# Attention decode gradients on one core: which DMA engines carry the rows of eight gradient stores

## The chip, the core and the metric

The kernel runs on one core of a Trainium2 chip. A core has a matrix engine (TensorE, PE in the profile, with its weight loads as PEld), a vector engine (VectorE, DVE), a scalar engine (ScalarE, ACT), a general engine (GpSimd, POOL), a queue engine (SyncE, SP) and 16 DMA engines that move data between the chip's memory (HBM) and the core's own memory of 128 partitions. SP and POOL issue DMAs here: SP's go through the queue that the profile names q1, POOL's through q0, and both queues feed the same 16 DMA engines.

The metric is the time on the device in microseconds, as the median of several runs. A profile of one execution shows its span, which is from the first to the last instruction.

## What is computed

For 2 x 32 = 64 heads, one query row attends to 8192 keys of 128 numbers in bf16. The reference takes the output and the gradients of q, k and v:

```
def _fwd_reference(q, k, v):
    scale = q.shape[-1] ** -0.5
    scores = jnp.einsum("bhqd,bhkd->bhqk", q, k) * scale
    p = _softmax(scores, axis=-1)
    return jnp.einsum("bhqk,bhkd->bhqd", p, v)
...
    _out, _vjp = jax.vjp(_f, q, k, v)
    _grads = _vjp(grad_out)
```

For one head that is, with the probabilities p and the incoming gradient g: the output p v; dv = p times g (an outer product, 8192 x 128); dp = v g; ds = p (dp - sum(p dp)); dq = scale ds k; dk = scale ds times q (again an outer product, 8192 x 128). K and V are read once (268 MB in all) and dk and dv are written once (268 MB).

## The kernel before

**Tiles.** Each head's K and V is one tile of 128 partitions, in which a partition holds 64 consecutive rows of 128 numbers, 16 KB. Twelve such tiles fit (`NTILE`, line 19), so six heads are in flight. `slot_of` (line 78) says which of the twelve places a tile takes: that of the tile which the head six places before it used, so `load(58, 0)`, K of head 58, goes where V of head 52 was, and `load(57, 1)` where K of head 51 was.

**Work on a head.** A tile is worked on in four chunks of 16 x 128 columns. PE transposes a chunk (line 184), ACT copies the result out (line 186), PE takes its product with q or with the incoming gradient (line 195). The softmax steps follow on DVE and ACT, PE sums up output and dq from the untransposed tiles (line 339), and then DVE writes dv over the V tile and dk over the K tile, chunk by chunk (`outer`, line 394). When the last chunk of a tile is done, its 2 MB are stored to HBM. The heads overlap: a step of the main loop holds transposes of one head and outer products of heads before it. dv of a head comes first, then dk of the same head four steps later, then dv of the next head. The order of instructions on each engine is fixed by the program (`pin`).

**Loads and stores.** All loads of K and V are issued by SP in that order (line 98). A load into a place waits, in SP's queue, until the store of the tile that used the place before has landed. Whole stores are issued by POOL (line 412) as one DMA of 128 rows; only the last head's go in quarters on SP. A whole load or store puts eight rows of 16 KB on each of the 16 DMA engines.

**Split stores.** `by_rows` (line 83) issues one store as several DMAs, each with a number of rows given in a list. In the kernel before, the dk stores of the eight heads in `SPREAD` (line 21: heads 4, 11, 18, 25, 32, 39, 46 and 53) go as 126 rows and 2 rows (line 409). At the start line 108 sets the place of POOL's DMAs among the engines back, and then a DMA of six rows of q is issued (line 110, `FIRST`). In the trace's list of packets each split store puts nine rows on fourteen engines and one row on the two others, in the place of eight on all sixteen; the change's words call these two engines 4 and 5.

Of the kernel before, what the change touches and what calls it, by code (L numbers as in the profile page):

```python
# [17 lines left out]
NG = 2  # L18
NTILE = 12
FIRST = 6  # L20
SPREAD = range(4, 60, 7)

@with_exitstack
def kernel(
# [12 lines left out]
    B, H, Sq, D = q.shape  # L38
    Sk = k.shape[2]
    P = nc.NUM_PARTITIONS  # L40
# [3 lines left out]
    NT = Sk // P  # L44
# [5 lines left out]
    load_eng = nc.sync  # L50
    store_eng = nc.gpsimd
    pin = tc.keep_in_program_order
# [30 lines left out]
    def by_rows(eng, dst, src, rows):  # L83

        p = 0
        for m in rows:
            pin(eng.dma_start(out=dst[p : p + m], in_=src[p : p + m], max_dma_last_dim=NT * D))
            p += m
# [15 lines left out]
    for w, a in enumerate((q, grad_out)):  # L104
        rows = a.rearrange("b h s d -> (b h s) d")
        r0 = FIRST if w == 0 else 0
        if r0:
# [3 lines left out]
                    out=qd_nat[:r0, w, :], in_=rows[:r0], max_dma_last_dim=D  # L111
# [276 lines left out]
    def outer(i, w, c, ends):  # L388

        h = heads[i]  # L390
        n0 = c * CH
        shape = [P, CH, D // 2, 2]
        pin(
            nc.vector.tensor_tensor(  # L394
                out=h.tile[w][:, n0 : n0 + CH, :].rearrange("p n (e t) -> p n e t", t=2),
                in0=h.qb[w][:]
                .rearrange("p (e t) -> p e t", t=2)
                .unsqueeze(1)
                .to_broadcast(shape),
                in1=h.pair[w][:, n0 : n0 + CH, :].unsqueeze(2).to_broadcast(shape),  # L400
                op=ALU.mult,
            )
        )
        if c + 1 in ends:
            at = ends.index(c + 1)
            b0, b1 = (ends[at - 1] if at else 0) * CH, (c + 1) * CH
            dst = (dv_v if w else dk_v)[i]
            if w == 0 and i in SPREAD:
                by_rows(store_eng, dst, h.tile[w], (P - 2, 2))
            else:  # L410
                eng = load_eng if len(ends) > 1 else store_eng
                pin(eng.dma_start(out=dst[:, b0:b1, :], in_=h.tile[w][:, b0:b1, :]))  # L412
# [10 lines left out]
    for g in range(SL * BH + O0 + NCH + 4 - SL):  # L423
# [15 lines left out]
        if x := within(O1):  # L439
            outer(x[0], 1, x[1], last if x[0] == BH - 1 else whole)  # L440
        if x := within(O0):
            outer(x[0], 0, x[1], last if x[0] == BH - 1 else whole)
        ev = None
        if g < SL * BH:
            i, r = divmod(g, SL)
# [74 lines left out]
```

## Time and profile before

| what | value |
|---|---|
| runs | 1284.86, 1285.96 and 1285.71 us, median 1285.71 |
| the profiled execution's own time | 1284.86 us |
| its span | 1283.1 us |
| PE, PEld, DVE, ACT busy | 88%, 67%, 73%, 76% of the span |
| POOL busy | 6% |
| HBM read and written | 268.47 MB and 268.47 MB, 418 GB/s over the span |
| whole stores by POOL (line 412) | 118, median 68.0 us from issue to landing |
| loads of a whole tile by SP (line 98) | 127, median 19.4 (V) and 19.7 us (K) |
| split stores by POOL (line 87) | 8 of 2016 KB (73.2 us) and 8 of 32 KB (72.6 us) |
| last head's stores by SP (line 412) | 8 of 512 KB, 22.1 us |

The time of a run is somewhat longer than the span, since it also holds what lies before the first and after the last instruction. Shares of busy time are means over the whole span. "From issue to landing" contains the time that a transfer waits behind others in its queue. The queues q8 and q14 carry the engines' own instructions.

### The profile page before, as it was taken

The page shows a single profiled execution, that of the slowest core. Times are in us where ns is not written, and L with a number is a line of the kernel's source. Part 1 is how long each engine was busy: PE and PEld are TensorE (multiplying, and loading weights), DVE is VectorE, ACT ScalarE, POOL GpSimd, SP SyncE. Part 2 cuts the span into 40 slices and gives each one's busy share as a digit, 9 for nine tenths or more (in the row PEclk, how much of TensorE's full clock was granted, in tenths as well). Part 3 has the DMA queues.
Part 4 walks back from the last instruction along what each step waited for, and adds up shares of the span by engine and source line. Part 5 has one row for each costly group of instructions (what it writes and reads, how often), then busy time and mean ns, then how long its engine had stood idle before and what let it go on. Part 6 is the DMA issues. An engine that isn't in the chain of part 4 may idle for free.

```text
span 1283.1 us, 42576 instructions
## 1 busy us (share of the span) xinstructions
PE 1128.5 (88%) x19268; PEld 859.1 (67%) x19268; DVE 935.2 (73%) x2122; ACT 975.2 (76%) x641; POOL 76.0 (6%) x143
## 2 busy tenths in 40 slices
PE   6999999999988998898889898898889888989881
PEld 5777777667666766676666676676667666667650
DVE  2888888778777777686777687786767677777773
ACT  6888888778877877787777787786778677778750
POOL 0000000000000000000000000000000000000000
PEclk9999999999999999998999999998989899899985
DMA  9999999999999999999999999999999999999996
GB/s 388 422 428 426 428 426 427 428 428 425 428 428 425 418 427 428 428 421 427 428 426 425 426 429 428 425 425 429 427 425 421 423 427 428 423 425 426 428 409 267
DMA packets 40194, 539.68 MB, mean 421 GB/s; under 512 B 5196, under 2 KB 5196, under 8 KB 6476
## 3 DMA queue, kind: packets, MB, share of 16 engines
q1 hardware_dynamic: 20172, 272.70, 50.0%
q0 software_dynamic: 19840, 264.25, 48.8%
q8 instruction: 150, 2.46, 0.7%
q14 instruction: 32, 0.26, 0.0%
HBM read 268.47 MB, written 268.47 MB: 418 GB/s over the span
## 4 chain that ended last, share of the span: by engine, by line
DMA 33%; another core or an unknown queue 29%; PE 16%; issue 10%; DVE 8%; ACT 1%; SPq 1%; POOL 1%; POOLq 0%; DVEq 0%; ACTq 0%
DMA kvt<-in_v_dram 20%; DMA out_dram<-kvt 7%; PE tp L184 7%; DVE kvt L394 5%; DMA kvt<-in_k_dram 5%; PE acc L339 4%; PE dpw L195 2%; PE sw L195 2%; DVE sel L362 1%; ACT ev L186 1%; SPq L98 1%; DMA qd_nat<-in_q_dram 1%; PE dpw L282 1%; POOL out_dram L412 0%
## 5 line engine op out<-in xcount | busy, mean ns | idle before, releaser
L186 ACT COPY ev<-tp 128x2048 bf16<-128x2048 bf16 x512 | 954.4, 1865 | 268.8 <-PE tp L184 256.8
L184 PE MATMUL tp<-ident_bf,kvt 128*128 128x128 bf16 x8192 | 558.5, 223 | 96.6 <-DMA kvt<-in_v_dram 74.4
L394 DVE TENSOR_TENSOR kvt<-qb,pair 128x2048 bf16<-128x2048 bf16 x512 | 621.2, 1214 | 0.3
L184 PEld LDWEIGHTS <-kvt 128*128 128x128 bf16 x8192 | 489.8, 101 | 103.6 <-DMA kvt<-in_v_dram 77.8
L195 PEld LDWEIGHTS <-ev 128*128 128x128 bf16 x8192 | 243.2, 96 | 208.7 <-issue 149.1
L339 PE MATMUL acc<-kvt,dS_pad 128*64 128x512 bf16 x1024 | 166.8, 408 | 0.8 <-DVE dqT L379 0.8
L339 PE MATMUL acc<-kvt,E_pad 128*64 128x512 bf16 x1024 | 160.5, 394 | 0.0
L195 PE MATMUL dpw<-qdT,ev 128*128 128x1 bf16 x4096 | 140.7, 164 | 18.8 <-DVE qb L177 18.0
L362 DVE SCALAR_TENSOR_TENSOR sel<-acc,diag,sel 128x128 f32<-128x128 f32 x384 | 134.7, 351 | 13.6
L195 PE MATMUL sw<-qdT,ev 128*128 128x1 bf16 x4096 | 141.8, 164 | 1.2 <-ACT ev L186 1.2
L207 DVE TENSOR_REDUCE mp<-sw 128x1 f32<-128x64 f32 x64 | 14.4, 224 | 156.1 <-PE sw L195 156.1
L412 POOL DMA_DIRECT2D out_dram<-kvt x118 | 63.3, 536 | 1086.1 <-DVE kvt L394 818.4
L339 PEld LDWEIGHTS <-dS_pad 128*64 128x64 bf16 x1024 | 37.4, 110 | 24.4 <-issue 5.3
L247 DVE CAST E_pad<-E_f 128x64 bf16<-128x64 f32 x64 | 12.5, 195 | 54.5 <-ACT E_f L238 54.5
L339 PEld LDWEIGHTS <-E_pad 128*64 128x64 bf16 x1024 | 36.4, 108 | 21.3 <-issue 0.7
L376 PE MATMUL acc<-ones,sel 128*128 128x1 f32 x256 | 43.5, 239 | 6.2 <-DVE sel L362 6.2
L253 DVE CUSTOM_DVE_ANT_0 junk<-E_f,dpw 128x64 bf16<-128x64 f32 x64 | 14.1, 221 | 45.3 <-PE dpw L195 45.3
L282 PE MATMUL dpw<-ld,ones 128*128 128x1 f32 x256 | 46.3, 250 | 0.1
L376 PEld LDWEIGHTS acc<-ones,sel 128*128 128x128 f32 x256 | 39.3, 194 | 7.3 <-DVE sel L362 7.3
L356 DVE TENSOR_SCALAR sel<-acc,diag 128x128 f32<-128x128 f32 x128 | 44.1, 344 | 0.0
L177 DVE CAST qb<-dpw 128x128 bf16<-128x128 f32 x128 | 35.4, 277 | 6.2 <-PE dpw L168 6.2
L282 PEld LDWEIGHTS dpw<-ld,ones 128*128 128x128 f32 x256 | 38.2, 188 | 0.5 <-DVE ld L253 0.5
(44 smaller groups left out, 314.2 us busy)
## 6 DMA issues: line engine op xcount, KB each, us to landing
out_dram<-kvt POOLq DMA_DIRECT2D x118, 2048.0 KB, 68.0
kvt<-in_v_dram SPq DMA_DIRECT2D x64, 2048.0 KB, 19.4
kvt<-in_k_dram SPq DMA_DIRECT2D x63, 2048.0 KB, 19.7
out_dram<-kvt POOLq DMA_DIRECT2D x8, 2016.0 KB, 73.2
out_dram<-kvt SPq DMA_DIRECT2D x8, 512.0 KB, 22.1
kvt<-in_k_dram SPq DMA_DIRECT2D x2, 512.0 KB, 4.5
kvt<-in_k_dram SPq DMA_DIRECT2D x1, 1024.0 KB, 7.3
out_dram<-kvt POOLq DMA_DIRECT2D x8, 32.0 KB, 72.6
```

Source lines behind the costliest of these rows:

```text
L177: pin(nc.vector.tensor_copy(out=h.qb[w][:], in_=h.qbp))
L184: pin(nc.tensor.transpose(tp[:, t, :], src[:, c * CH + t, :], ident_bf[:]))
L186: pin(nc.scalar.copy(out=ev[:], in_=tp[:]))
L195: nc.tensor.matmul(dst[:, c * CH + t : c * CH + t + 1], lhsT=ev[:, t, :], rhs=qdT[:, w, i : i + 1], start=True, stop=True,)
L207: pin(nc.vector.reduce_max(out=h.mp[:], in_=h.s, axis=AX.X))
L282: nc.tensor.matmul(out, lhsT=ones[:].to_broadcast([P, P]), rhs=col, start=True, stop=True)
L339: nc.tensor.matmul(h.acc[w][g : g + CW, :], lhsT=wts[:, n0 : n0 + CW], rhs=rows[:, n0 : n0 + QT, :].rearrange("p n d -> p (n d)"), start=( ...
L356: nc.vector.tensor_scalar(out=h.sel[:], in0=block, scalar1=diag[:, 0:1], scalar2=None, op0=ALU.mult)
L362: nc.vector.scalar_tensor_tensor(out=h.sel[:], in0=block, scalar=diag[:, b : b + 1], in1=h.sel[:], op0=ALU.mult, op1=ALU.add,)
L376: nc.tensor.matmul(h.acc[w][:, 0:1], lhsT=h.sel[:], rhs=ones[:], start=True, stop=True)
L394: nc.vector.tensor_tensor(out=h.tile[w][:, n0 : n0 + CH, :].rearrange("p n (e t) -> p n e t", t=2), in0=h.qb[w][:] .rearrange("p (e t) -> ...
L412: pin(eng.dma_start(out=dst[:, b0:b1, :], in_=h.tile[w][:, b0:b1, :]))
```

## The change

The number of split dk stores goes from eight to six (heads 5, 14, 23, 32, 41 and 50), each still 126 rows and 2 rows. The dv store of head 52 is split into 9, 95 and 22 rows on POOL and 2 rows on SP; the dv store of head 55 into 95 and 33 rows on POOL. By the words of the change, the 95 rows go to engines 15 and 0 to 3, and the split dk stores leave out engines 4 and 5. All bytes are moved as before, and nothing else differs.

```
-SPREAD = range(4, 60, 7)
+SHIFT = (52, 55)
+SPREAD = range(5, 52, 9)
...
-            if w == 0 and i in SPREAD:
+            if w == 1 and i == SHIFT[0]:
+                by_rows(store_eng, dst, h.tile[w], (9, 95, 22))
+                pin(load_eng.dma_start(out=dst[P - 2 :], in_=h.tile[w][P - 2 :], max_dma_last_dim=NT * D))
+            elif w == 1 and i in SHIFT:
+                by_rows(store_eng, dst, h.tile[w], (95, 33))
+            elif w == 0 and i in SPREAD:
                 by_rows(store_eng, dst, h.tile[w], (P - 2, 2))
```

On POOL's queue the DMAs stand in the order of the code: after the split store of head 50 two whole stores (dv and dk of head 51), then the 9, 95 and 22 rows, five whole stores, the 95 and 33 rows, and whole stores to the end. On SP's queue the store of the last 2 rows of dv of head 52 stands after `load(57, 1)` and before `load(58, 0)`. The other engines' instructions are the same, in the same order.

## The prediction

> **What bounds the kernel now.** First the page's slices and its DMA queues.
>
> ```profile
> span 1283.1 us, 42576 instructions
> ...
> DMA  9999999999999999999999999999999999999996
> ...
> q1 hardware_dynamic: 20172, 272.70, 50.0%
> q0 software_dynamic: 19840, 264.25, 48.8%
> q8 instruction: 150, 2.46, 0.7%
> q14 instruction: 32, 0.26, 0.0%
> ```
>
> The 16 DMA engines are full in 39 of 40 slices, so the kernel is bound by bytes through them, and as they share work unevenly, by the engine that has most. Queue q1 (loads, from SP) moves 272.70 MB in 50.0% of 16 x 1283.1 us: 0.617 us for a row of 16 KB. In the list of packets the median row takes 0.611 us on both queues; I use that. The 150 instruction fetches of q8, 16 KB each, take 0.98 us in the list (147 us in all).
>
> Second, the busy time by windows at the end (the last two columns are the DMA share and GB/s).
>
> ```profile
> 1238.00:1248.00 10.00, 8.45 (x130) 5.99 (x130) 8.53 (x21) 5.90 (x5) 0.53 (x1) 0.96 0.88 372
> 1248.00:1262.00 14.00, 7.37 (x30) 3.08 (x30) 12.63 (x25) 0.00 (x0) 0.00 (x0) 0.50 0.99 414
> 1262.00:1266.00 4.00, 0.00 (x0) 0.00 (x0) 0.04 (x1) 0.00 (x0) 0.00 (x0) 0.50 0.69 285
> 1266.00:1268.00 2.00, 0.00 (x0) 0.00 (x0) 0.00 (x0) 0.00 (x0) 0.00 (x0) 0.50 0.51 213
> 1268.00:1274.00 6.00, 0.00 (x0) 0.00 (x0) 0.00 (x0) 0.00 (x0) 0.00 (x0) 0.50 0.52 217
> 1274.00:1280.00 6.00, 0.00 (x0) 0.00 (x0) 0.00 (x0) 0.00 (x0) 0.00 (x0) 0.50 0.44 180
> 1280.00:1283.00 3.00, 0.00 (x0) 0.00 (x0) 0.00 (x0) 0.00 (x0) 0.00 (x0) 0.50 0.10 36
> ```
>
> All compute ends by 1262. Then a share of 0.69, 0.52 and 0.44 of 16 engines is 11, 8 and 7 engines: seven work to 1280 on stores while nine have run dry. That tail of 18 us is what the change can shorten.
>
> Third, which engines are the seven? The list of packets has start, duration, size and queue, but no engine. On one engine a row starts 3 to 4 ns before the recorded end of the row before it, and each whole transfer puts eight rows and a 4-byte completion on an engine; with both rules the packets chain into 16 lines. Their last packets end at 1279.9 to 1281.0 (seven lines), 1274.4, 1268.1, 1266.2, 1263.4 and 1262.4 to 1262.6 (five). The chains also show:
> - The q8 fetches go round eight lines in turn: 150/8 x 0.98 = 18.4 us for each. Seven of those lines are the late seven (1280.5 - 1262.4 = 18 us); the eighth is one of the two that the split stores relieve.
> - A split store of 126 + 2 rows (line 87) gives 14 lines nine rows, as 18 half rows, and two lines one. These two I call 4 and 5, as the change does; the first six q rows (line 110) touched six lines, among them these two, so the other four are engines 0 to 3. None of the four is a fetch line.
> - One line that isn't a PE fetch line takes a q14 packet at 112.8, 179.3, 250.5, 316.3 and 383.8 us and so on (0.33 us each, 16 by 1130 us: PE's 38,536 instructions in q8's 2.46 MB are 64 B each, so VectorE's 2122 make 16.6 such packets of 8 KB) and 12 us of longer rows, where other lines have 3 to 7. At 1130 us it leads the seven by 8.5 rows, 5.2 us: 1280.5 - 5.2 = 1275.3, so it is the line that ends at 1274.4. It chains back to one of the six lines with a q row, and not to a relieved one. So it is one of engines 0 to 3.
> The last point is the weakest: lines whose packets end within 1 ns of each other can be exchanged.
>
> **The change, part by part.** Rows are counted against a whole store's eight for each engine.
>
> Split dk stores, eight to six: before, engines 4 and 5 had -56, the others +8; now -42 and +6.
>
> dv store of head 52: 9 rows go one each to engines 6 to 14; 95 rows, by the change's own words, to five engines, 19 each; 22 rows two each to 4 to 14; SP's last 2 rows to two engines. That is -5 for 6 to 14, +11 for 15 and 0 to 3, about -6 for 4 and 5. Head 55 (95 and 33): -5 for 4 to 14, +11 for the five.
>
> Sum, after less before: engines 6 to 14 go from +8 to -4, so -12 rows, -7.3 us. Engines 15 and 0 to 3 go from +8 to +28, so +20 rows, +12.2 us. Engines 4 and 5 go from -56 to about -53, +2 us; both lead (the slower of them ends near 1263.4). SP's two rows add one row, 0.6 us, to two engines that I leave open. -108 + 100 + 6 + 2 = 0.
>
> The trace shows 126 and 2 rows on 14 and 2 engines, not 95. Bounds: on all 16 (six each, as whole stores spread) the dv parts give almost nothing; on five, 19 each. I take five, by the nearest row (126 went to 14, its largest divisor up to 16; that of 95 is 5). [...]
>
> New ends: the late seven 1281.0 - 7.3 = 1273.7. Of the five, lines that ended at 1262.4 to 1263.4: 1274.6 to 1275.6. The line that ended at 1268.1, if it is one of them: 1280.3. The q14 line: 1274.36 + 12.2 = **1286.6**, 5.5 us behind today's last packet. That engine is busy throughout, so nothing hides its extra rows.
>
> [...] Here one line, with 45 us of long rows by 1131 us, stands out, and it is a relieved one; the trace can't name its number. [...]
>
> Waits. Loads wait in SP's queue for the store that frees their tile:
>
> ```profile
> SPq L98 <- DMA out_dram<-kvt: 1139.0, 116, 25.1
> ...
> 1034.47 0.53 POOL L412 DMA_DIRECT2D out_dram<-kvt  x1 [4.58 <-DVE kvt L394]
> ...
> 1094.06 0.53 POOL L412 DMA_DIRECT2D out_dram<-kvt  x1 [8.54 <-DVE kvt L394]
> ...
> 1093.66 0.33 SPq L98 DMA_DIRECT2D kvt<-in_v_dram  x1
> ...
> 1103.29 0.33 SPq L98 DMA_DIRECT2D kvt<-in_k_dram  x1
> ```
>
> Counting back from the split store of head 53 at 1064.97, the POOL rows are the dv stores of heads 52 and 55. In the new order SP's two-row store stands between load(57, 1) and load(58, 0). It can't leave before load(57, 1), which waits for dk of head 51 (1093.66), and it then runs behind that load's eight rows: at best 8 x 2 x 0.611 + 1 = 11 us with stores interleaved, at worst the 19.4 us of a load plus 1.2. load(58, 0), which left at 1103.29, is 1 to 11 us later; I take 5. Behind it in SP's queue wait all later loads, and for them PE's transposes of head 58. The cover is the store queue: a store takes 68 us to land, the engines stay full until 1238, and heads run at 17.3 us early on (the chain's DVE steps at 37.1, 54.4, 71.7) against 20 later (loads at 1043.5 and 1204.0, eight heads), so compute makes up 2.7 us a head, 13 in the last five. It costs nothing at the end; without the cover, 5. On POOL the split costs three more issues at 0.58 to 0.78 us, in gaps of 4.6 to 10 us: nothing. dv of head 55 lands late on the q14 line by about 11 rows, 7 to 14 us, and holds load(61, 0) as long; the last SP stores then leave at 1259 plus up to 14, 1273, still before 1285, so this too lies under that engine's work.
>
> Sum: own time of the profiled execution 1284.86 + 5.5 = 1290.4 (span 1288.6). The median of the runs lies 0.85 above that execution: 1285.71 + 5.5 = **1291.2**.
>
> **The rivals.**
> - Faster: neither the q14 line nor the one that ended at 1268.1 is among the five. Then 1275.6 is last: 1285.71 - 5.4 = 1280.3. For it: five lines have 18 us of room, and the fetch lines are seven of 6 to 14. Against: only two of the seven unrelieved lines without PE fetches lie outside the five, and the chain puts the q14 line inside.
> - Same: only the 1268.1 line is among the five (1280.3: -0.7, 1285.0), or the 95 rows spread over 16 engines and the change does little of what it says (six spread stores for eight and 7 or 8 rows for each: -1 or -2 us, 1284).
> - Slower still: the late load and the late store of heads 52 and 55 hold up the last heads beyond the cover, so that the q14 engine runs dry before the last stores come. It decides once the last SP store leaves after 1285 (its eight quarter rows an engine, 0.159 us each, need 1.3 us before 1286.6), 26 us later than now; the 14 above and 10 more from the first wait with no cover would just not do. It adds what is over, 1 to 3: 1293.
>
> **How the numbers follow.** Forecast 1291.2, chance 0.67; slower still 0.06; same 0.12; faster 0.15. A change below 0.2% (2.6 us) can't be told from none here. Slower by more is then 0.73. Own range of the forecast: 1289 to 1293 (one row more or less, long rows on the five engines of 1 us, the start's 0.5). From 1283, where the same case ends, to 1294, the range leaves out most of the faster case.
>
> **What would show it.** Right: at the end one or two engines (share 0.06 to 0.13) work alone for some 6 us or more past 1281, where now seven do. The late seven gone from the tail by 1274. SP's two-row store leaving near 1094 and load(58, 0) after it. Wrong: a tail in which 12 or more engines end together near 1275, or seven still working near 1279.

## The result, and the profile after

| | before | after |
|---|---|---|
| median of the runs (range, number) | 1285.99 us (1284.86 to 1291.3, 6) | 1295.62 us (1292.04 to 1297.34, 6) |
| ratio, 95% interval | | 1.0065 [1.0042, 1.0088] |
| profiled execution: own time, span | 1284.86, 1283.1 us | 1296.8, 1295.0 us |

The change makes the kernel slower, by 8.4 us by the ratio and 9.6 us by the medians. The profiled execution of after lies 1.2 us above the median of its runs. The forecast was 1291.2 us with a range up to 1294: the direction came true, the size did not.

The page of after, in the lines that answer to those of before, with the GB/s of each slice added:

```profile
span 1295.0 us, 42582 instructions
...
GB/s 387 422 428 427 425 426 429 427 427 427 427 427 427 428 427 426 421 428 428 428 425 428 427 427 428 427 418 426 426 427 428 428 403 391 390 422 411 427 411 207
...
q1 hardware_dynamic: 20178, 272.74, 49.6%
q0 software_dynamic: 20624, 264.22, 48.8%
q8 instruction: 150, 2.46, 0.7%
```

The shares of the queues are almost those of before although the span is 12 us longer, so the same bytes have taken more time of the DMA engines. The GB/s show where: slices 33 to 35 (32.4 us each, 1036 to 1133 us) hold the two split dv stores and have 403, 391 and 390 GB/s, where the slices beside them have 428 and 422. The busy time by windows says whether the engines ran dry there (last two columns: DMA share and GB/s). First before, then after:

```profile
1060.00:1090.00 30.00, 26.21 (x465) 20.03 (x465) 21.80 (x54) 22.89 (x17) 2.49 (x4) 1.00 1.01 427
```

```profile
1060.00:1090.00 30.00, 26.94 (x455) 20.43 (x452) 22.30 (x53) 22.33 (x16) 2.19 (x4) 0.94 0.98 378
```

The share falls by 3%, the bytes by 11%. Most of the loss is therefore not idle time: the engines are busy with rows that take longer. From 1030 to 1190 us the list of packets has, before and after, a mean of 619 and 656 ns for the 16 KB rows of the store queue, 314 and 368 ns for its half rows, and 613 and 619 ns for the rows of the loads.

The end of after, by windows:

```profile
1248.00:1262.00 14.00, 10.48 (x152) 7.14 (x151) 12.39 (x30) 6.56 (x6) 0.53 (x1) 0.94 0.94 397
1262.00:1268.00 6.00, 4.07 (x19) 1.45 (x14) 5.89 (x10) 0.00 (x0) 0.00 (x0) 0.50 0.98 410
1268.00:1274.00 6.00, 0.90 (x3) 0.63 (x3) 3.61 (x9) 0.00 (x0) 0.00 (x0) 0.50 0.99 406
1274.00:1280.00 6.00, 0.00 (x0) 0.00 (x0) 0.00 (x0) 0.00 (x0) 0.00 (x0) 0.50 0.61 245
1280.00:1286.00 6.00, 0.00 (x0) 0.00 (x0) 0.00 (x0) 0.00 (x0) 0.00 (x0) 0.50 0.17 69
1286.00:1290.00 4.00, 0.00 (x0) 0.00 (x0) 0.00 (x0) 0.00 (x0) 0.00 (x0) 0.50 0.06 24
1290.00:1295.00 5.00, 0.00 (x0) 0.00 (x0) 0.00 (x0) 0.00 (x0) 0.00 (x0) 0.50 0.05 18
```

All 16 engines have work to 1273, when before eight had run dry, and from 1286 a share of 0.06 is one engine alone, to 1293. The packets of after, chained into 16 lines as in the prediction, say which. The last line ends at 1293.3. It takes a q14 packet at 112.7, 179.2 and 251.6 us, so it is the q14 line, and 184 half rows: 6 x 18 of the split dk stores and 38 + 38, that is 19 + 19 rows of the two dv stores. Four other lines carry 184 half rows too and end at 1275.7 to 1279.8; the PE fetch lines carry 120 (108 + 6 + 6). As in the prediction, lines whose packets end within 1 ns of each other can be exchanged in such a chain.

SP's queue in after (start, length, line):

```profile
1097.28 0.33 SPq L99 DMA_DIRECT2D kvt<-in_v_dram  x1
1097.70 0.73 SPq L411 DMA_DIRECT2D out_dram<-kvt  x1
1114.75 0.35 SPq L99 DMA_DIRECT2D kvt<-in_k_dram  x1
...
1152.02 0.33 SPq L99 DMA_DIRECT2D kvt<-in_v_dram  x1
1178.90 0.33 SPq L99 DMA_DIRECT2D kvt<-in_k_dram  x1
```

`load(58, 0)`, the third row, left at 1103.29 before: 11.5 us late. `load(61, 0)`, the last row, has a gap of 27 us ahead of it. POOL's queue (in brackets the idle time before an instruction, and what ended it):

```profile
1045.51 1.03 POOL L88 DMA_DIRECT2D out_dram<-kvt  x1 [11.38 <-issue]
1052.66 0.58 POOL L88 DMA_DIRECT2D out_dram<-kvt  x1 [6.12 <-DMA out_dram<-kvt]
1063.37 0.58 POOL L418 DMA_DIRECT2D out_dram<-kvt  x1 [10.13 <-DMA out_dram<-kvt]
1078.30 1.08 POOL L418 DMA_DIRECT2D out_dram<-kvt  x2 [14.35 <-DMA out_dram<-kvt]
```

The 95 rows, the 22 rows and the next stores: three of these four rows wait for an older store to land. dk of head 52, the third row, left at 1044.98 before, and the two stores of head 53, the last row, at 1053.83 and 1064.97: they leave 18, 24 and 13 us late.

### The profile page after: what moved, and what is told of

It is laid out like the page before. It is cut to its first block, busy times and chain, and to the rows that moved or that the text cites. A ratio compares the mean times of both kernels' runs of the same rounds, so it can differ in the third digit from the quotient of the medians.

```text
span 1295.0 us, 42582 instructions
## 1 busy us (share of the span) xinstructions
PE 1127.1 (87%) x19268; PEld 857.3 (66%) x19268; DVE 935.5 (72%) x2122; ACT 975.8 (75%) x641; POOL 77.1 (6%) x144
## 4 chain that ended last, share of the span: by engine, by line
DMA 36%; another core or an unknown queue 30%; PE 19%; DVE 7%; issue 4%; ACT 1%; SPq 1%; POOL 0%; DVEq 0%; POOLq 0%; ACTq 0%
DMA kvt<-in_v_dram 22%; PE tp L185 9%; DMA out_dram<-kvt 7%; DMA kvt<-in_k_dram 6%; PE acc L340 5%; DVE kvt L395 4%; PE sw L196 2%; PE dpw L196 2%; DVE sel L363 1%; SPq L99 1%; ACT ev L187 1%; PE dpw L283 1%; DMA qd_nat<-in_q_dram 1%; DVE sel L357 0%
## 5 line engine op out<-in xcount | busy, mean ns | idle before, releaser
L208 DVE TENSOR_REDUCE mp<-sw 128x1 f32<-128x64 f32 x64 | 14.4, 225 | 144.3 <-PE sw L196 144.3
```

What stands on the lines that cost most here:

```text
L208: pin(nc.vector.reduce_max(out=h.mp[:], in_=h.s, axis=AX.X))
```

## The experiments

Four theories were set against each other. A: only the number of rows on the most loaded engine counts (the prediction's sum). B: rows take longer while a store is on its way whose rows are dealt out otherwise than a whole store's. C: the load that SP's two-row store holds back costs the rest. D: each DMA more costs, since POOL has only some stores in flight (eight, by its waits in the run with 8 x 16 rows below).

Two sums from the list of packets go with every run. "Longer rows": the time of each packet above the usual one (0.611 us for 16 KB, 0.309 for 8 KB, 0.159 for 4 KB), summed over the trace, by 16. "Idle": the time in which fewer than 16 engines have a packet, from 50 us to the end of the first line, by 16. Since all kernels move the same bytes, the mean end of the 16 lines can move only by such sums; the last line's end over that mean is the unevenness, which is what A counts. These sums and ends come from one execution of each kernel; the runs of before alone go from 1284.7 to 1292.5 us, so a difference of about 1 us in them decides nothing.

| kernel | ratio to before, 95% interval | mean end of the 16 lines | longer rows, idle (less before's) | last line over the mean |
|---|---|---|---|---|
| before | 1 | 1271.8 | 0, 0 | 9.2 |
| after | 1.0065 [1.0042, 1.0088] | 1278.9 (+7.1) | +6.1, +0.8 | 14.4 |
| six splits only | 0.9985 [0.9976, 0.9994] | 1271.1 (-0.7) | -1.4, +0.7 | 9.0 |
| head 52 only | 1.0003 [0.9989, 1.0016] | 1275.7 (+3.9) | +3.2, +0.6 | 8.2 |
| 112 + 16 rows | 1.0025 [1.001, 1.004] | 1276.1 (+4.3) | +2.7, +1.6 | 8.4 |
| 8 x 16 rows | 1.0034 [1.0025, 1.0043] | 1281.8 (+10.0) | +3.9, +6.1 | 4.6 |
| two rows on ACT | 1.0096 [1.0066, 1.0126] | 1278.7 (+6.9) | +4.5, +1.9 | 16.9 |
| pairs of half rows | 0.9995 [0.9981, 1.0009] | 1272.3 (+0.5) | -0.8, +1.1 | 11.5 |
| odd counts | 1.0111 [1.0064, 1.0157] | 1284.4 (+12.6) | +4.9, +6.1 | 16.3 |
| late shift | 1.002 [1.0006, 1.0034] | 1276.1 (+4.3) | +2.3, +2.1 | 10.2 |
| 64 + 64 rows, ten stores | 1.0402 [1.0364, 1.044] | 1319.8 (+48.0) | +38.5, +9.0 | 17.2 |
| two half widths, ten stores | 1.0055 [1.0035, 1.0075] | 1275.9 (+4.0) | +4.4, -0.6 | 10.3 |

The two sums give the shift of the mean to within 0.5 us in all rows but the odd counts.

**Six splits only.** Before with the six splits of after; all dv stores are whole.

```
-SPREAD = range(4, 60, 7)
+SPREAD = range(5, 52, 9)
```

> Only the first part of the change: six split dk stores (heads 5 to 50), dv stores of heads 52 and 55 whole. Theory A (time is the rows on the most loaded engine, 0.611 us each): the seven late lines and all others carry 2 rows less, so the last packet goes from 1281.0 to 1279.8 and the time from 1285.7 to 1284.5. Theory B (rows of the two split dv stores, and rows beside them, take longer than 0.611 us; some 100 engine-us in the changed kernel): the same, as no dv store is split. Theory C (SP's two-row store and the late loads set the extra time): the same. A time over 1288 would speak against all three: then the six splits themselves cost.

Measured: 1284.2 us against 1285.83. Its end, by windows:

```profile
1262.00:1268.00 6.00, 0.00 (x0) 0.00 (x0) 0.00 (x0) 0.00 (x0) 0.00 (x0) 0.50 0.58 241
1268.00:1274.00 6.00, 0.00 (x0) 0.00 (x0) 0.00 (x0) 0.00 (x0) 0.00 (x0) 0.50 0.52 219
1274.00:1280.00 6.00, 0.00 (x0) 0.00 (x0) 0.00 (x0) 0.00 (x0) 0.00 (x0) 0.50 0.41 165
1280.00:1283.00 3.00, 0.00 (x0) 0.00 (x0) 0.00 (x0) 0.00 (x0) 0.00 (x0) 0.50 0.01 4
```

The tail is before's, with the late lines gone by 1280.2 in place of 1281.0. A holds within the noise: by it, two split stores less take two rows, 1.2 us, from fourteen lines, and the last line ends 0.9 us sooner. This is also the one version that is clearly faster than before, by 0.15%.

**Head 52 only.** The dv store of head 55 is whole again.

```
-SHIFT = (52, 55)
+SHIFT = (52,)
```

> Six split dk stores and the dv split of head 52 alone (9, 95, 22 rows, 2 on SP); dv of head 55 whole. A: the seven lines -7 rows (1276.7), the q14 line +9 rows, 1274.4 + 5.5 = 1279.9, alone at the end: 1284.6. B: half of the longer rows, about 3 us on every line: the q14 line at 1283, the time 1287.7. C: load(58, 0) leaves some 10 us late as in the changed kernel; if that wait is what cost the 7 us missing in the sum, the time is 1289 or more and the longer rows appear only when the loads are late.

Measured: 1286.76 us. One dv split moves the mean end by 3.9 us, about half of after's 7.1 (against the six splits alone, by 4.6 of 7.8). The longer rows of the store queue begin in 1060 to 1080 (27 engine-us, 2 to 4 in a usual 20 us), before SP's two-row store leaves near 1097: C can't have made these.

**112 + 16 rows.** Before, with dv of head 52 as 112 rows on POOL and 16 on SP: by the expectation's count seven rows and one row on each of the 16 engines, so no engine should get more than in a whole store.

```
+            if w == 1 and i == 52:
+                by_rows(store_eng, dst, h.tile[w], (112,))
+                pin(load_eng.dma_start(out=dst[112:], in_=h.tile[w][112:], max_dma_last_dim=NT * D))
```

> Kernel before, with dv of head 52 as 112 rows on POOL and 16 rows on SP, 7 rows and 1 row for each of the 16 engines: the wait in SP's queue without any shift of rows. A: no shift, 1285.7. B: 1285.7, at most 1 more. C: load(58, 0) leaves some 10 us late, as in the changed kernel, rows get longer around 1110 us, and the time is 1288 to 1292.

Measured: 1289.51 us, mean end +4.3. `load(58, 0)` left at 1116.76, as late as in after, so this run left C beside B. B's own expectation, at most 1 us more, was missed too: 2.7 of the 4.3 us are longer rows, though by the count each engine has as many rows as of a whole store (the last line ends 8.4 us over the mean, 9.2 in before).

**8 x 16 rows.** Before, with dv of heads 52 and 55 as eight DMAs of 16 rows.

```
+            if w == 1 and i in (52, 55):
+                by_rows(store_eng, dst, h.tile[w], (16,) * 8)
```

> Kernel before, with dv of heads 52 and 55 each as eight DMAs of 16 rows on POOL: every engine still carries 8 rows of each store, but reads them from other partitions than in a whole store, and in half rows. A: 1285.7. B, if rows take longer because engines read partitions that others use: 1288 to 1292 with 50 to 100 engine-us of longer rows between 1030 and 1190. B, if rows take longer because few engines carry many rows: 1285.7 and no longer rows.

Measured: 1290.33 us. Here D shows itself; POOL's queue:

```profile
1044.86 0.50 POOL L87 DMA_DIRECT2D out_dram<-kvt  x1 [8.18 <-DMA out_dram<-kvt]
1054.63 0.50 POOL L87 DMA_DIRECT2D out_dram<-kvt  x1 [9.27 <-DMA out_dram<-kvt]
1064.28 0.50 POOL L87 DMA_DIRECT2D out_dram<-kvt  x1 [9.16 <-DMA out_dram<-kvt]
1075.47 0.50 POOL L87 DMA_DIRECT2D out_dram<-kvt  x1 [10.69 <-DMA out_dram<-kvt]
```

Each piece waits about 10 us until an older store has landed, whatever its own size. In the trace's records POOL's DMAs use eight semaphores in turn (101 to 108), and each of these pieces waits for the semaphore that it is to use itself, the first for 103: so for the DMA eight places before it. That number belongs to this program; no run shows a limit of the chip. Eight small DMAs bring one store's bytes, and the engines run dry for 104 engine-us in 1050 to 1100. Longer rows come on top, over the trace most of them in the load queue: 100 engine-us in 1030 to 1190, where before has 22. The 78 between them lie in the 50 to 100 that B expected if the partitions count; by the other form of B, few engines with many rows, there should have been none. That an engine reads other partitions here is the expectation's reading: the list of packets names no partition. In after the two heads have three DMAs more on POOL and there is little idle time (+0.8), so D is real and small there.

**Two rows on ACT.** After, with the two-row store issued by the scalar engine, so that SP's loads aren't behind it.

```
-                pin(load_eng.dma_start(out=dst[P - 2 :], in_=h.tile[w][P - 2 :], max_dma_last_dim=NT * D))
+                pin(nc.scalar.dma_start(out=dst[P - 2 :], in_=h.tile[w][P - 2 :], max_dma_last_dim=NT * D))
```

> The changed kernel with SP's two-row store issued by ACT instead, so that no load waits behind it in SP's queue; rows and engines as in the changed kernel. A (only rows count) and B (longer rows beside the 95-row stores): 1295.6 as the changed kernel. C (the load held back in SP's queue makes rows longer or lines idle): load(58, 0) leaves some 10 us earlier than 1114.7 and the time is 1292 to 1293. D (POOL can have some eight stores on their way, so each further DMA of a split store makes the next wait for an old one to land: dk of head 52 left 18 us late, at 1063): the stores of POOL leave as late as in the changed kernel, and most of the extra time stays.

Measured: 1299.15 us, not less than after. Its lone line in the last window:

```profile
1290.00:1297.00 7.00, 0.00 (x0) 0.00 (x0) 0.00 (x0) 0.00 (x0) 0.00 (x0) 0.50 0.05 19
```

`load(58, 0)` left at 1110.96, 4 us sooner where some 10 were expected, and nothing was won. C falls as the main cause of the loss: where the load leaves sooner the mean end stays at +6.9, and 8 x 16 rows has longer rows with no store on SP's queue.

**Pairs of half rows.** Before, with dv of heads 52 and 55 through `by_rows` as one DMA of 128 rows, which cuts each row in two as every split store does.

```
+            if w == 1 and i in (52, 55):
+                by_rows(store_eng, dst, h.tile[w], (P,))
```

> Kernel before with dv of heads 52 and 55 as one DMA each of 128 rows, cut in half rows as the split stores are: same engines, same partitions, same number of DMAs. All of A to D: 1285.7. If half rows themselves cost time, longer halves show and the time is 1286.5 to 1288.

Measured: 1286.71 us against 1286.42; longer rows as before. It isn't the cutting in two.

**Odd counts.** Six splits, and dv of head 52 in counts of which all but the 9 are primes above 16. In line with 126 rows on 14 lines and 95 on five, the expectation takes one engine for each of these, so that five engines get 17, 19, 23, 29 and 31 rows.

```
+            if w == 1 and i == 52:
+                by_rows(store_eng, dst, h.tile[w], (9, 17, 19, 23, 29, 31))
```

> Six split dk stores, and dv of head 52 as 9 rows and then 17, 19, 23, 29 and 31 rows, each a prime and so on one engine: 15, 0, 1, 2 and 3 get different numbers. In the trace each of these lines can be told by its half rows (142, 146, 154, 166, 170 in all). A: the line with the q14 packets every 70 us ends alone at 1278.7 if it is engine 15, 1279.9 for 0, 1282.3 for 1, 1286.0 for 2, 1287.2 for 3. B and D add 3 to 6 on all lines; D: six DMAs in place of one hold POOL back by 30 us or more, and lines idle.

Measured: 1302.55 us (two runs), with lines that end at 1300.7 and 1296.2 and the others by 1286. The mark was to tell the engine number of the q14 line; the packets of this trace could not be chained safely back to the start, so the number stays open, and that each prime went to one engine isn't shown. Of the mean's shift of 12.6 us, 1.6 are in neither sum. Most of that is packets of 4 bytes: the list has 8435 against before's 4931, and 3504 of 9 ns each, which overlap the packet before by 3 to 4 ns, are some 1.2 us for each line.

**Late shift.** Six splits, and dk of head 62 dealt out so that, by the expectation's count, rows go from late lines to early ones when the loads are done.

```
+            if w == 0 and i == BH - 2:
+                by_rows(store_eng, dst, h.tile[w], (7, 81, 7, 27, 6))
```

> Six split dk stores, dv of heads 52 and 55 whole, and the last store of POOL (dk of head 62, after the last load) as 7, 81, 7, 27 and 6 rows: 2 or 3 rows for the late engines 6 to 12, 12 or 13 for the nine others. A: the seven late lines end 5 rows, 3.1 us, before those of the kernel with six splits (1280.2 to 1277.1), the q14 line at 1275.6: 1281.2. B: rows are not longer here, as no loads run any more. D: the pieces wait on POOL for old stores to land, which at the end costs up to 5 us: 1281 to 1286.

Measured: 1290.29 us, against 1284.2 of the six splits alone (1.002 and 0.9985 of before, each beside its own runs of before). In the windows of its end the engines are full and the bytes are not (before has a share of 0.99 with 414 GB/s in 1248 to 1262):

```profile
1248.00:1254.00 6.00, 4.07 (x18) 1.57 (x18) 5.86 (x12) 0.00 (x0) 1.44 (x3) 0.50 0.96 339
1254.00:1262.00 8.00, 3.61 (x14) 1.81 (x14) 6.78 (x12) 0.00 (x0) 0.00 (x0) 0.50 0.97 336
```

The last row of a load ended at 1232.8. So rows get longer beside an odd split without any load running too, against what B expected here.

**64 + 64 rows against two half widths.** The runs so far vary several things at once. These two have the same number of DMAs, the same bytes in each, the same number of packets (41634 in each trace) and, by the count, the same eight rows' worth on each engine; what differs is whether a DMA takes half of the rows or half the width of all rows, and with it which addresses of the HBM are written together. That an engine then gets other rows is the author's reading: the list of packets names no row. In both, ten dv stores of before (heads 30, 33 to 57) are sent in two parts.

```
+            if w == 1 and i in range(30, 60, 3):
+                by_rows(store_eng, dst, h.tile[w], (64, 64))
```

> Kernel before, with ten dv stores (heads 30, 33 to 57) sent as rows 0 to 63 and rows 64 to 127: two DMAs that should put four rows each on all 16 engines, so every engine still has its eight rows per store, but most rows are read by another line than in a whole store. Only the rows an engine gets and the number of DMAs (one more per store) change. Theory A (only the number of rows on the most loaded engine counts): 1285.7, packet times normal. Theory B (rows are longer in a store whose rows are dealt out otherwise than in a whole store): the 112 + 16 split cost 39 engine-us of longer rows for one store and the 8 x 16 split about 20 to 35 each, so ten stores 200 to 400 engine-us, 12 to 25 us on the end if it falls on all lines: 1293 or more. Theory D (each further DMA costs a place in flight at POOL): the same time as the run with two half-width DMAs.

```
+            if w == 1 and i in range(30, 60, 3):
+                pin(store_eng.dma_start(out=dst[:, : NT // 2], in_=h.tile[w][:, : NT // 2]))
+                pin(store_eng.dma_start(out=dst[:, NT // 2 :], in_=h.tile[w][:, NT // 2 :]))
```

> Kernel before, with the same ten dv stores sent as two DMAs of all 128 rows, each half a row wide: as many DMAs as in the 64 + 64 run and the same rows on the same lines as in a whole store. Theory A: 1285.7. Theory B: 1285.7 to 1286.5, packet times normal (half rows alone cost nothing in the run of half-row pairs). Theory D: above 1287 and as much as the 64 + 64 run.

Measured: 1337.91 and 1290.9 us against 1285.27. The split by rows costs 52.6 us, the split by width 5.6. The page of the first, then of the second:

```profile
DMA  9999999999999999999999999999999999999984
GB/s 390 422 427 426 426 427 427 428 427 426 428 427 421 425 428 428 425 425 426 423 408 379 381 391 343 402 355 417 398 420 379 398 411 415 402 385 399 409 372 179
```

```profile
DMA  9999999999999999999999999999999999999996
GB/s 388 425 428 425 427 426 428 426 427 425 428 429 423 418 426 427 428 423 425 426 426 428 425 426 426 418 412 420 426 421 403 419 426 426 420 421 427 425 424 262
```

The first of the ten stores leaves at 591 us, in slice 18. Up to slice 20 the two kernels are alike; from slice 21 on the first drops to between 343 and 420 GB/s, with the engines at nine tenths or more up to slice 38. Between 550 and 1250 us its half rows take 390 ns in the mean, 14% of them over 400 ns (320 ns and 3% in the split by width, 315 ns and 1% before), and the loads beside them 631 ns (615 and 613). That is B without A, C or D: at an equal number of DMAs and packets it is the split by rows that has the long rows. That the cause is which rows an engine carries is the author's inference from that. Whether the time is lost where the tile is read or where the HBM is written, no run separates. The split by width bounds D to 0.56 us for each further DMA. It missed its own expectation of no change: its 5.6 us are longer rows too (+4.4), not idle time (-0.6), and for these no theory here has a reason.

## Why the prediction was wrong

**What held.** The bound by the DMA engines, the unevenness of the 16 lines and the counting of rows. The lines with 184 and 120 half rows are the forecast five with 19 rows from each of the two 95-row DMAs, and the engines 6 to 14 with three and three rows: the 95 rows went to five engines, 19 each, as the prediction took it from the 126 rows on 14, and not to all 16, its other bound. (The numbers of the engines are the change's words: the list of packets names no engine.) The q14 line is one of the five and ends alone. In the prediction's numbers that line was to end at 1286.6, which is 14.8 us over before's mean end of 1271.8. It ended 14.4 over the mean of after, and 16.9 in the run with two rows on ACT, which moves the same rows: the term for the unevenness was right to some 2 us, and its agreement to half a microsecond is in part luck.

**The step that failed** is the price of a row: 0.611 us for each, also for rows of a store that is cut at 9, 104 and 126 or at 95, and for the rows beside them. The sum gave a change of zero for all 16 lines together (-108 + 100 + 6 + 2 = 0 rows), so their mean end was to stay at 1271.8. It went to 1278.9. Of these 7.1 us, 6.1 are longer rows and 0.8 idle time. So the last line's 12.3 us (1281.0 to 1293.3) are 7.1 of the mean, forecast as 0, and 5.2 of unevenness, forecast as 5.5. Against the six splits alone the two dv splits cost the mean 7.8 us, 4.6 with head 52 and 3.2 more with head 55. The q14 line had its share: its packets on the store queue were some 10 us longer than usual between 1030 and 1190, where in the same length of time from 500 us it is about 1. For "long rows on the five engines" the range had 1 us, too little by some 6. (One reading of the prediction was off without weight: a q14 packet takes 0.31 us in the list, not 0.33.)

**The late seven** were to end at 1273.7 with -12 rows each. The lines with fetches in after end between 1273.3 and 1284.9. Three of them (1281.8, 1283.2, 1284.9) end later than any line did before, with twelve rows less on them, which the count of rows can't give.

**SP's wait.** `load(58, 0)` left 11.5 us late, past the end of the forecast 1 to 11. The cover held, as forecast: SP's last eight stores leave from 1259.27 to 1270.32, before the 1273 named for them and long before the last line's end, and the run that moved the two-row store off SP's queue was no faster. `load(61, 0)` had a gap of 27 us, where 7 to 14 over the usual 10 were forecast; no run sets its cost apart.

**POOL.** That three more issues fit into gaps and cost nothing was wrong as a step: the 22 rows and the next stores waited 6 to 14 us each, since in this program a DMA of POOL waits for the one eight places before it to land. The price in after stays within the 0.8 us of idle time.

**The rivals.** The faster and the same one rested on the q14 line being elsewhere, or on the 95 rows spread over 16 engines; the line counts exclude both. The slower one named the last stores leaving after 1285; they left by 1270. The time went past its 1293, but by another mechanism.

**What makes the rows longer** is shown as far as this: it goes with how a store is cut (ten stores cut at row 64 cost 52.6 us, cut at half their width 5.6), it needs no load beside it (339 and 336 GB/s at a share of 0.96 and 0.97 in the late shift), and it falls on other packets too, those of whole stores (619 to 656 ns between 1030 and 1190 us, before and after) and of loads (613 to 631 ns in the kernel with 64 + 64 rows). What the rows then wait for is not shown: the author's guess is the side where the tile is read, and a cause on the side of the HBM stays open beside it.

## What to carry to other kernels

A kernel bound by the DMA engines has two separate accounts: the mean end of the 16 lines, which is the total time of all packets and of the idle time between them, and the distance of the last line from it. Moving rows between engines by odd row counts is meant to shorten the second, and here it lengthened the first: the two 95-row splits cost the mean of all lines 7.8 us, more than the 1.6 us of time that fewer split stores gave back. Keep whole 128-row transfers where the engines are full, split by width where a store must be split (ten such splits cost 5.6 us here, ten at row 64 52.6), and price a split by a trace that has one of the same kind: a half row took 315 ns in the mean in before and 390 in the kernel with 64 + 64 rows.

## What the runs showed of the hardware

- How a store is cut changes the time of a row, at an equal number of DMAs and packets: 390 ns in the mean for a half row in the kernel with 64 + 64 rows, 320 ns in the one with two half widths; before has 315 ns (550 to 1250 us). The rows of loads in flight beside them rose from 613 to 631 ns.
- A store dealt out in odd counts brings more packets of 4 bytes: the list has 8435 in the kernel with odd counts, 5721 in after, 4931 in before, 9 ns each.
- Engine instructions are an uneven load: the 150 fetches of 0.98 us go round eight of 16 lines, and seven of these end 16 to 19 us after the first lines in before and in the kernel with six splits.
